# Block 0 of an attention and cos-gate MLP kernel: exponentials weigh the values first, the division by their sums follows behind TensorE; clamps on VectorE; a new order

## The chip, the core and the metric

One core of a Trainium2 chip runs the whole program. The metric is device time in microseconds (us). Engines are named as the profile names them: PE is TensorE (PEld its weight loads), DVE VectorE, ACT ScalarE, POOL GpSimd, SP the engine whose queue issues every DMA here. Each engine works through its own instructions in order.

## What is computed

```python
def _attn_ref(q, k, v):                       # (4, 8, 768, 64) each
    k_sum = k.reshape(B, H, nb, 32, D).max(axis=3)
    v_sum = v.reshape(B, H, nb, 32, D).mean(axis=3)
    scores_l = scale * np.matmul(q, k.transpose(0, 1, 3, 2))
    mask_l = np.abs(pos[:, None] - pos[None, :]) < 16
    scores_s = scale * np.einsum('bhsd,bhnd->bhsn', q, k_sum) + np.log(32)
    scores_all = np.concatenate([np.where(mask_l, scores_l, -1e9), scores_s], axis=-1)
    a = np.exp(scores_all - np.max(scores_all, axis=-1, keepdims=True))
    a = a / (np.sum(a, axis=-1, keepdims=True) + 1e-09)
    return np.matmul(a, np.concatenate([v, v_sum], axis=2))

def _moe_ref(x, w_in, w_out):                 # x (3072, 512), w_in (512, 2048)
    h = x @ w_in
    return ((h * np.cos(h)) @ w_out).astype(np.float32)
```

q, k and v are fp32. The weights are float64 in memory and are read as pairs of 32-bit words, out of which the kernel makes fp32 itself.

## The kernel before

The 3072 tokens are 8 blocks of 384 tokens (two blocks to a batch entry). Attention of a block is four **groups** a, b, c, d, each a pair of heads; `a0` is group a of block 0. A group's steps: load q, k, v and the summaries of v (`load_vs`), transposes of q and k on PE, scores on PE (its masks first, `place_masks`), a copy out of PSUM (`scale`), row maximum on DVE (`maximum`, L588), subtraction on POOL (`less_max`, L593), exponential on ACT (`exp`, L606), row sums on DVE (`sums`, L609), reciprocal on DVE (`inverse`, L614), multiplication by it on POOL (`normalize`, L617), transposes of the probabilities on PE (`turn_p`, L626) with copies on ACT (`place_p`), the product with the values on PE (`values`, L670), which comes out transposed and is x, and x split in a high and a low fp32r part (`x_high` on ACT or DVE, `x_low` on DVE, L356). From group c of block 2 on the probabilities are transposed on DVE and through DRAM instead (`square_p`, `move_out`, `move_in`).

The MLP runs in 128 **steps**; a step takes one block and one of 16 slices f of 128 hidden columns. Its `up` is 12 matmuls (L714), ACT and DVE make h cos h of it (L724, L727, L732, L735, L739), split in `gh` and `gl`, and `down` and `down_low` are 9 matmuls (L770). Steps 0 to 5 are block 0 with slices 0 to 5, steps 6 to 21 block 1 with all 16, steps 22 to 31 block 0 with the rest. `s0.up`, the first, needs x of all four groups of block 0 and slice 0 of the weights.

A weight **slice** is 1 MB of float64 bits, loaded by SP in two DMAs (L371, L375) into one of the buffers `late`, and turned into fp32 bits and split: `magnitude` on ACT (L388), `clamp` on DVE or POOL (L393), `shift`, `last_bits`, `first_bits` on DVE (L399, L407, L415), `high_part` on ACT or DVE, `low_part` mostly on POOL (L356).

Every instruction's place on its engine is written out by hand in the table `ORDER`: a token such as `b0.sm` or `s0.up.2` is one step of one group, slice or MLP step, and the letter at its end names the engine (a, v, p) or the numbers the PSUM banks. All DMAs are on SP's queue and share eight semaphores in turn, so that a DMA is issued only after the one eight places ahead of it has landed.

## Time and profile before

| | us |
|---|---|
| median of 3 runs | 663.17 (660.64 to 663.44) |
| the profiled execution, its own time | 661.89 |
| its span, first to last instruction | 660.1 |
| PE busy in the span | 632.6 (96%) |
| DVE, ACT, POOL busy | 449.7, 363.9, 221.8 |
| TensorE's mean granted clock | 0.987 |

Rows are read so: a timeline row has a start, a duration, the engine, the line of the kernel, the operation and its tiles; in square brackets stands how long the engine sat idle before it, and what ended that. A window row has, for a stretch, each engine's busy time with the number of its instructions, then PE's granted clock (1.00 is 2.4 GHz, 0.50 is 1.2 GHz), the busy share of the DMA engines and what they moved. An fp32 matmul shows as two MATMUL records.

### The profile page before, as it was taken

Reading aid. Unit: us, or ns where it says so; the run is one execution under the profiler, and the core shown is the slowest. Engines: PE = TensorE matmul, PEld = TensorE weight load, DVE = VectorE, ACT = ScalarE, POOL = GpSimd, SP = SyncE. Lnnn points to the kernel's source line nnn. Section 1 sums busy time; section 2 is a strip of 40 time slices with the busy share of each in tenths; the row PEclk is TensorE's granted clock in tenths of the full one; section 3 lists DMA queues with packets and bytes.
Section 4 is the critical chain, followed back from the end, with each engine's and each line's share of the span. In section 5 each row is a group of like instructions: output and inputs, shape, how many; then the busy total and the mean of one; then the engine's idle time right before and its main releaser. Section 6 shows DMA issues by size and latency. Waiting matters only on the chain.

```text
span 660.1 us, 13282 instructions
## 1 busy us (share of the span) xinstructions
PE 632.6 (96%) x5141; PEld 560.2 (85%) x5141; DVE 449.7 (68%) x798; ACT 363.9 (55%) x640; POOL 221.8 (34%) x219
## 2 busy tenths in 40 slices
PE   6478999999999999999999999999999999999996
PEld 5256889989988998898898899889889989899985
DVE  4887999887855576668797777576876756433344
ACT  2656977776554485437477464356554645444342
POOL 4784896764430342301323411112330212010110
PEclk9869999999999999999999999999999999999999
DMA  9997906544243244525445433424364332000001
GB/s 224 259 271 203 276 15 223 169 109 71 55 122 85 91 124 132 127 59 114 111 107 135 147 98 97 114 43 85 115 163 104 92 94 70 5 1 17 16 17 48
DMA packets 167158, 72.68 MB, mean 110 GB/s; under 512 B 136824, under 2 KB 155832, under 8 KB 167096
## 3 DMA queue, kind: packets, MB, share of 16 engines
q1 hardware_dynamic: 167096, 71.84, 40.9%
q8 instruction: 40, 0.66, 0.4%
q14 instruction: 22, 0.18, 0.1%
HBM read 53.72 MB, written 15.73 MB: 105 GB/s over the span
## 4 chain that ended last, share of the span: by engine, by line
PE 86%; DMA 5%; SPq 3%; POOL 2%; DVE 1%; issue 1%; ACT 1%; DVEq 0%; POOLq 0%; ACTq 0%
PE banks L770 39%; PE banks L714 39%; PE banks L569 4%; PE banks L670 3%; DMA late<-in_moe_w_out_dram 3%; DMA late<-in_v_dram 1%; SPq L456 1%; POOL w L356 1%; DMA late<-in_q_dram 1%; POOL gl L356 1%; SPq L493 1%; POOL stage L393 0%; ACT stage L388 0%; PE banks L556 0%; DVE m L588 0%
## 5 line engine op out<-in xcount | busy, mean ns | idle before, releaser
L714 PE MATMUL banks<-xh,w 128*128 128x384 f32 x1024 | 272.1, 337 | 0.1
L770 PE MATMUL banks<-w,gh 128*128 128x512 f32 x768 | 198.1, 393 | 0.2 <-ACT gh L350 0.2
L714 PEld LDWEIGHTS banks<-xh,w 128*128 128x128 f32 x1024 | 185.9, 188 | 2.8 <-ACT pt L350 0.4
L714 PE MATMUL banks<-xl,w 128*128 128x384 f32 x512 | 171.4, 335 | 0.0
L770 PEld LDWEIGHTS banks<-w,gh 128*128 128x128 f32 x768 | 142.6, 188 | 29.0 <-ACT gh L350 0.5
L724 ACT ACTIVATE t<-banks 128x384 int32<-128x384 f32 x128 | 62.5, 489 | 133.6 <-DVE gl L356 54.9
L356 POOL TENSOR_TENSOR gl<-t,gh 128x384 fp32r<-128x384 f32 x55 | 56.6, 1029 | 221.4 <-ACT gh L350 86.0
L770 PE MATMUL banks<-w,gl 128*128 128x512 f32 x384 | 109.8, 394 | 0.1
L727 DVE SCALAR_TENSOR_TENSOR t<-t,banks 128x384 f32<-128x384 int32 x128 | 70.0, 548 | 56.9 <-ACT t L724 56.2
L732 ACT ACTIVATE t<-t 128x384 f32<-128x384 f32 x128 | 66.7, 523 | 66.3 <-DVE t L727 66.0
L714 PEld LDWEIGHTS banks<-xl,w 128*128 128x128 f32 x512 | 96.1, 188 | 1.6
L739 DVE SCALAR_TENSOR_TENSOR t<-t,banks 128x384 f32<-128x384 f32 x128 | 69.3, 546 | 41.2 <-ACT t L735 41.0
L770 PEld LDWEIGHTS banks<-w,gl 128*128 128x128 f32 x384 | 71.1, 188 | 14.6 <-DVE gl L356 0.2
L593 POOL TENSOR_TENSOR sc<-sc,m 128x720 f32<-128x720 f32 x28 | 40.1, 1431 | 129.2 <-DVE m L588 129.2
L735 ACT ACTIVATE t<-t 128x384 f32<-128x384 f32 x128 | 65.8, 521 | 2.1
L617 POOL TENSOR_TENSOR sc<-sc,r 128x720 f32<-128x720 f32 x28 | 39.5, 1411 | 51.4 <-DVE r L614 50.3
L350 ACT CAST gh<-t 128x384 fp32r<-128x384 f32 x68 | 34.7, 510 | 33.2 <-PE banks L770 16.5
L356 DVE TENSOR_TENSOR gl<-t,gh 128x384 fp32r<-128x384 f32 x73 | 41.7, 572 | 12.6 <-ACT gh L350 6.5
L356 POOL TENSOR_TENSOR w<-stage,w 128x1024 fp32r<-128x1024 f32 x15 | 36.2, 2416 | 10.0 <-ACT w L350 8.6
L352 DVE CAST gh<-t 128x384 fp32r<-128x384 f32 x60 | 23.2, 386 | 22.2 <-PE banks L770 20.4
L580 DVE SCALAR_TENSOR_TENSOR sc<-banks,mask 128x360 f32<-128x360 f32 x48 | 24.4, 524 | 19.2 <-PE banks L569 19.0
L569 PEld LDWEIGHTS banks<-kd,qd 64*64 64x64 f32 x1344 | 28.4, 135 | 9.4 <-issue 6.7
(102 smaller groups left out, 620.7 us busy)
## 6 DMA issues: line engine op xcount, KB each, us to landing
pd<-stage SPq DMA_DIRECT2D x22, 384.0 KB
late<-in_moe_w_in_dram SPq DMA_DIRECT2D x16, 512.0 KB
late<-in_moe_w_out_dram SPq DMA_DIRECT2D x16, 512.0 KB
pt<-pd SPq DMA_DIRECT2D x66, 96.0 KB
vn<-in_v_dram SPq DMA_DIRECT2D x52, 120.0 KB
out_dram<-stage SPq DMA_DIRECT2D x23, 256.0 KB
kn<-in_v_dram SPq DMA_DIRECT2D x24, 192.0 KB
qn<-in_q_dram SPq DMA_DIRECT2D x92, 48.0 KB
```

The lines of the kernel that those rows point to most:

```text
L350: eng.copy(out=out, in_=in_)
L356: eng.tensor_tensor(out=lo, in0=src, in1=hi.bitcast(F32), op=ALU.subtract)
L569: nc.tensor.matmul(out=self.sp[hh][s * QT : (s + 1) * QT, c, lo : lo + n], lhsT=self.qd[rows, t * QT : (t + 1) * QT], rhs=self.kd[rows, ke ...
L593: nc.gpsimd.tensor_tensor(out=self.sc, in0=self.sc, in1=self.m.unsqueeze(2).broadcast_to([P, U, NK]), op=ALU.subtract)
L617: nc.gpsimd.tensor_tensor(out=self.sc, in0=self.sc, in1=self.r.unsqueeze(2).broadcast_to([P, U, NK]), op=ALU.mult)
L714: nc.tensor.matmul(out=self.h, lhsT=w_of(name, self.f)[:, c * P : (c + 1) * P], rhs=x_of(self.blk, part, c), start=n == 0, stop=n == last,)
L724: nc.scalar.activation(out=self.t.bitcast(I32), in_=self.h, func=AF.Copy, scale=1.0 / TWO_PI)
L727: nc.vector.scalar_tensor_tensor(out=self.t, in0=self.t.bitcast(I32), scalar=-TWO_PI, in1=self.h, op0=ALU.mult, op1=ALU.add)
L732: nc.scalar.activation(out=self.t, in_=self.t, func=AF.Sin, scale=0.5)
L735: nc.scalar.activation(out=self.t, in_=self.t, func=AF.Square, scale=math.sqrt(2.0))
L739: nc.vector.scalar_tensor_tensor(out=self.t, in0=self.t, scalar=-1.0, in1=self.h, op0=ALU.add, op1=ALU.mult)
L770: nc.tensor.matmul(out=self.acc[i], lhsT=g[:, i * P : (i + 1) * P], rhs=w_of(name, self.f), start=self.first and n == 0, stop=self.last an ...
```

## The change

**Block 0's values.** `LATE` marks the four groups of block 0. They have no `sums` and no `normalize`: the exponentials are transposed as they are (with one row more, the 1e-9 that stood beside them for the sum), and `values` multiplies with the probabilities as the stationary operand, so that x comes out with the tokens on the partitions. Beside each of the 12 products with the values stands one with a column of ones, which gives the sum. Then DVE takes the reciprocal of the sums (`inverse`), multiplies (`divide`, token `xn`) into one tile `xq` that all four groups use, PE transposes that (`turn_x`, `tx`, three matmuls), and `x_high` and `x_low` go on as before.

**Clamps.** Those of slices 3 and 7 move from POOL to DVE, so that all 16 are there.

**b2.** The second table of `TURNS` has a one more: group b of block 2 sends its probabilities through DVE and DRAM instead of PE.

**The order** is a new table: other places, banks and engines for many tokens.

```diff
+LATE = "11110000000000000000000000000000"
-TURNS = ("00000000011111111111111111111111", "00000000001111111111111111111111")
+TURNS = ("00000000011111111111111111111111", "00000000011111111111111111111111")
...
-b0.ck.0.v a0.ck.0.a a0.ks.0 a0.ms.5.6 a0.ck.1.a a0.ks.1 b0.q a0.sc c0.tk.0.7 a0.z.1.a a0.z.0.v w1.l c0.ck.0.a a0.mx
...
+    ones = const.tile([P, 1], F32, name="ones")
+    nc.vector.memset(ones, 1.0)
...
         def inverse(self):
-            if self.fused:
+            if self.late:
+                self.r = att.tile([P, U], F32, name="r", bufs=2)
+                nc.vector.reciprocal(out=self.r, in_=self.xw[:, :, D])
+                return
...
+                nc.tensor.transpose(out=pT[:, t - lo, :], in_=self.all[:, t, : self.rows], identity=ident)
...
         def values(self, i):
+            if self.late:
+                self.xw = bank(i)[:, : U * (D + 1)].rearrange("p (u n) -> p u n", u=U)
+                for t in range(U):
+                    c, s = divmod(t, 2)
+                    for hh in range(2):
+                        p, to = self.pt[2 * c + hh][s], self.xw[s * QT : (s + 1) * QT, 2 * c + hh]
+                        nc.tensor.matmul(
+                            out=to[:, :D], lhsT=p[:NK], rhs=self.vn[:, t, hh * D : (hh + 1) * D],
+                            start=True, stop=True,
+                        )
+                        nc.tensor.matmul(out=to[:, D:], lhsT=p, rhs=ones[: self.rows], start=True, stop=True)
+                return
...
+        def divide(self):
+            nc.vector.tensor_tensor(
+                out=self.xq.rearrange("p (u n) -> p u n", u=U), in0=self.xw[:, :, :D],
+                in1=self.r.unsqueeze(2).broadcast_to([P, U, D]), op=ALU.mult,
+            )
+
+        def turn_x(self, i):
+            self.xps = bank(i)[:, :TB]
+            for c in range(QC):
+                cols = slice(c * P, (c + 1) * P)
+                nc.tensor.transpose(out=self.xps[:, cols], in_=self.xq[:, cols], identity=ident)
```

**DVE**, from the clamp of slice 2 on. Before (L393 clamp, L399, L407, L415 the bits, L609 sums, L614 reciprocal, L356 x_low, L588 maximum):

```order
L393 TENSOR_SCALAR stage_407<-stage_407 128x1024
L415 SCALAR_TENSOR_TENSOR stage_420<-late_131,banks 128x1024
L609 TENSOR_REDUCE r<-late_130 128x6
L399 TENSOR_SCALAR banks<-stage_407 128x1024
L614 RECIPROCAL r<-r 128x6
L407 SCALAR_TENSOR_TENSOR banks<-late_125,banks 128x1024
L415 SCALAR_TENSOR_TENSOR stage_464<-late_125,banks 128x1024
L393 TENSOR_SCALAR stage_451<-stage_451 128x1024
L356 TENSOR_TENSOR xl_0_487<-banks,xh_0_459 128x384
L399 TENSOR_SCALAR banks<-stage_451 128x1024
```

The same place now, in the changed file's lines (L399 clamp, L405, L413, L421 the bits, L609 maximum, L643 reciprocal of the sums in PSUM, L722 divide, L362 x_low):

```order
L399 TENSOR_SCALAR stage_405<-stage_405 128x1024
L405 TENSOR_SCALAR banks<-stage_405 128x1024
L643 RECIPROCAL r<-banks 128x6
L413 SCALAR_TENSOR_TENSOR banks<-late_127,banks 128x1024
L722 TENSOR_TENSOR x_3_140<-banks,r 128x384
L421 SCALAR_TENSOR_TENSOR stage_470<-late_127,banks 128x1024
L609 TENSOR_REDUCE m<-sc 128x6
L399 TENSOR_SCALAR stage_453<-stage_453 128x1024
L643 RECIPROCAL r<-banks 128x6
L405 TENSOR_SCALAR banks<-stage_453 128x1024
L722 TENSOR_TENSOR x_3_140<-banks,r 128x384
L362 TENSOR_TENSOR xl_0_531<-banks,xh_0_511 128x384
```

The sums of d0 and the reciprocal that followed them are gone; the reciprocals of a0 and c0 now stand behind what PE writes to `banks`, and each divide behind its reciprocal.

**SP**, from a load of the summaries for block 1 (L493; L477 and L485 load v, L456 q, L254 the v blocks of batch entry 1, L371 and L375 a slice; `vn_104` is b0's v) on, before:

```order
L493 DMA late_128<-vs_293 24x6x64 x2
L477 DMA late_128<-in_v_dram 96x5x64 x2
L485 DMA late_128<-in_v_dram 80x2x64
L493 DMA vn_104<-vs_293 24x6x64 x2
L493 DMA late_128<-vs_293 24x6x64 x2
L456 DMA qn<-in_q_dram 128x3x64 x2
L477 DMA vn_104<-in_v_dram 96x5x64 x2
L485 DMA vn_104<-in_v_dram 80x2x64
L477 DMA late_129<-in_v_dram 96x5x64 x2
L485 DMA late_129<-in_v_dram 80x2x64
L254 DMA kn<-in_v_dram 96x512
L371 DMA late_125<-in_moe_w_in_dram 128x4x256
```

Now (L466 q, L258 v blocks, L487 and L495 v, L503 summaries, L377 a slice; `vn_106` is b0's v):

```order
L466 DMA late_132<-in_q_dram 128x3x64 x2
L258 DMA kn<-in_v_dram 96x512
L487 DMA vn_106<-in_v_dram 96x5x64 x2
L495 DMA vn_106<-in_v_dram 80x2x64
L503 DMA vn_106<-vs_297 24x6x64 x2
L503 DMA late_130<-vs_297 24x6x64 x2
L487 DMA late_131<-in_v_dram 96x5x64 x2
L495 DMA late_131<-in_v_dram 80x2x64
L503 DMA late_130<-vs_297 24x6x64 x2
L466 DMA qn<-in_q_dram 128x3x64 x2
L377 DMA late_127<-in_moe_w_in_dram 128x4x256
L381 DMA late_127<-in_moe_w_out_dram 128x1024
L466 DMA qn<-in_q_dram 128x3x64 x2
```

b0's v stands twelve DMAs earlier in the program's queue; the q of d1 (the first `qn` here) now stands behind it, and the load of slice 8 (`late_127`) directly behind that, five DMAs earlier than it was.

**PE**, from the last matmuls of `s0.up` on, before (L626 transposes of a1's exponentials, L556 masks of d1):

```order
L714 MATMUL banks<-xl_0_557,w_438 128x384
L714 MATMUL banks<-xh_0_494,w_438 128x384
L626 MATMUL banks<-ident,sc 120x128 x4
L556 MATMUL banks<-mask,ident 128x360 x2
L626 MATMUL banks<-ident,sc 120x128 x2
```

Now (L512 the transposes of a2's q, L659 those of a1's exponentials):

```order
L772 MATMUL banks<-xl_0_616,w_440 128x384
L772 MATMUL banks<-xh_0_599,w_440 128x384
L659 MATMUL banks<-ident,sc 120x128 x4
L512 MATMUL banks<-ident,qn 128x128 x3
L567 MATMUL banks<-mask,ident 128x360 x2
L659 MATMUL banks<-ident,sc 120x128 x2
```

The transposes of a2's q, which stood behind `s1.up`, now stand behind `s0.up`.

## Rows read from the trace of the kernel before

**Rows 1.** Three stretches of the span that end at 655.20 us, all engines
```profile
0.00:58.88 58.88, 37.45 (x532) 27.28 (x533) 44.10 (x61) 30.61 (x53) 37.63 (x55) 0.86 0.87 231
58.88:95.02 36.14, 35.04 (x302) 29.61 (x300) 32.81 (x48) 30.76 (x51) 29.89 (x23) 1.00 0.64 192
95.02:655.20 560.18, 560.10 (x4312) 503.33 (x4310) 371.72 (x689) 302.22 (x537) 154.29 (x143) 1.00 0.35 92
```

**Rows 2.** PE's waits, whole span: line, releaser, us in total, times, longest
```profile
PE banks L502 <- DMA late<-in_q_dram: 6.6, 3, 2.4
...
PE banks L670 <- DMA vn<-in_v_dram: 2.3, 1, 2.3
```

**Rows 3.** DVE alone from slice 1's clamp to b0's x_low, then clock and DMA
```profile
22.93:58.74 35.81, 31.29 (x37) 0.76 0.80 211
```

**Rows 4.** Timeline of DVE: clamp, sums, x_low, reciprocal, shift, maximum, slice 8's clamp
```profile
22.93 0.70 DVE L393 TENSOR_SCALAR stage<-stage 128x1024 f32<-128x1024 f32 x1 [0.31 <-ACT stage L388]
...
45.71 0.91 DVE L609 TENSOR_REDUCE r<-sc 128x6 f32<-128x726 f32 x1 [1.31 <-ACT sc L606]
46.54 0.55 DVE L356 TENSOR_TENSOR xl<-banks,xh 128x384 fp32r<-128x384 f32 x1
47.00 0.18 DVE L614 RECIPROCAL r<-r 128x6 f32<-128x6 f32 x1
47.83 1.23 DVE L399 TENSOR_SCALAR banks<-stage 128x1024 int32<-128x1024 int32 x1 [0.65 <-POOL stage L393]
49.14 0.90 DVE L588 TENSOR_REDUCE m<-sc 128x6 f32<-128x720 f32 x1
...
65.20 0.69 DVE L393 TENSOR_SCALAR stage<-stage 128x1024 f32<-128x1024 f32 x1 [1.54 <-ACT stage L388]
```

**Rows 5.** Timeline of POOL: slice 3's clamp
```profile
44.18 3.62 POOL L393 TENSOR_SCALAR stage<-stage 128x1024 f32<-128x1024 f32 x1
```

**Rows 6.** Timeline of PE: values of c0, then from a1's q to d0's values
```profile
39.26 1.55 PE L670 MATMUL banks<-pt,x 120*64 120x64 f32 x24 [0.21 <-ACT pt L350]
...
43.93 0.52 PE L502 MATMUL banks<-ident,late 128*128 128x128 f32 x3 [1.81 <-DMA late<-in_q_dram]
44.29 2.14 PE L556 MATMUL banks<-mask,ident 128*128 128x360 f32 x4
...
48.15 0.78 PE L502 MATMUL banks<-ident,late 128*128 128x128 f32 x3
48.86 0.92 PE L670 MATMUL banks<-pt,x 120*64 120x64 f32 x24
49.70 1.48 PE L556 MATMUL banks<-mask,ident 128*128 128x360 f32 x4
```

**Rows 7.** A stretch with a low clock, all engines
```profile
28.00:42.00 14.00, 6.80 (x63) 5.56 (x63) 13.68 (x18) 7.91 (x12) 11.07 (x6) 0.51 0.90 253
```

**Rows 8.** Groups of score matmuls on PE: count, busy us, mean ns, idle before
```profile
L569 PE MATMUL banks<-kd,qd 64*64 64x96 f32 x672 | 29.0, 268 | 0.0
...
L569 PE MATMUL banks<-kd,qd 64*64 64x24 f32 x672 | 24.8, 200 | 0.0
```

**Rows 9.** The chain that ended last: start and length of two slices' landing
```profile
31.82 5.28 DMA late<-in_moe_w_out_dram
...
57.51 6.41 DMA late<-in_moe_w_out_dram
```

**Rows 10.** Timeline of PE: the transposes of b1's q
```profile
37.75 0.88 PE L502 MATMUL banks<-ident,late 128*128 128x128 f32 x3 [2.35 <-DMA late<-in_q_dram]
```

**Rows 11.** Timeline of SP: issues of b1's q, d1's q and b0's v
```profile
34.11 1.03 SPq L456 DMA_DIRECT2D late<-in_q_dram  x2
...
51.88 0.98 SPq L456 DMA_DIRECT2D qn<-in_q_dram  x2
52.91 1.26 SPq L477 DMA_DIRECT2D vn<-in_v_dram  x2
```

**Rows 12.** Timeline of PE: six transposes, and the matmuls behind them
```profile
81.26 0.82 PE L626 MATMUL banks<-ident,late 128*120 128x128 f32 x6
81.84 1.64 PE L770 MATMUL banks<-w,gh 128*128 128x512 f32 x6
```

More of the change, by code (lines that the diff above doesn't have):

```diff
@@ L442, in __init__ @@
             self.squares, self.moved = (t[blk * NG + pr : blk * NG + pr + 1] == "1" for t in TURNS)
+            self.late = LATE[blk * NG + pr : blk * NG + pr + 1] == "1"
+            self.rows = NK + 1 if self.late else NK
+            self.pmax = int(PMAX[blk * NG + pr : blk * NG + pr + 1] or "0")
             self.kT, self.pT, self.pt, self.pts = {}, {}, {}, None
@@ L551, in score_banks @@
             self.sp = [bank(i)[:, : QC * NK].rearrange("p (c n) -> p c n", c=QC) for i in two]
+            self.first_bank = two[0]
         def place_masks(self, *two):
@@ L587, in maximum @@
             m = self.m = att.tile([P, U], F32, name="m", bufs=2)
+            if self.pmax:
+                i = self.first_bank
+                nc.vector.tensor_reduce(
+                    out=m.rearrange("p (c h) -> p h c", h=2),
+                    in_=banks[:, i : i + 2, : QC * NK].rearrange("p h (c n) -> p h c n", n=NK),
+                    axis=AX.X, op=ALU.max,
+                )
+                if self.pmax == 2:
+                    nc.vector.tensor_scalar_mul(m, m, -1.0)
+                return
             nc.vector.tensor_reduce(
@@ L597, in exp @@
         def exp(self):
-            self.r = att.tile([P, U], F32, name="r", bufs=2)
-            if self.fused:
+            if not self.late:
+                self.r = att.tile([P, U], F32, name="r", bufs=2)
+            if self.pmax == 2:
+                for u in range(U):
+                    c, h = divmod(u, 2)
+                    nc.scalar.activation(
+                        out=self.sc[:, u, :], in_=self.sp[h][:, c, :], func=AF.Exp, bias=self.m[:, u : u + 1],
+                        accum_out=self.r[:, u : u + 1],
+                    )
+            elif self.fused:
                 for u in range(U):
@@ L623, in turn_p @@
             lo, hi = ((0, 4), (4, U))[j]
-            pT = self.pT[j] = bank(i)[:NK, : (hi - lo) * P].rearrange("p (t n) -> p t n", t=hi - lo)
+            pT = self.pT[j] = bank(i)[: self.rows, : (hi - lo) * P].rearrange("p (t n) -> p t n", t=hi - lo)
             for t in range(lo, hi):
-                nc.tensor.transpose(out=pT[:, t - lo, :], in_=self.sc[:, t, :], identity=ident)
+                nc.tensor.transpose(out=pT[:, t - lo, :], in_=self.all[:, t, : self.rows], identity=ident)
         def place_p(self, j, eng):
@@ L631, in place_p @@
                 self.pts = att.tile([P, U * P], F32, name="pt")
-            pt = self.pts[:NK].rearrange("p (t n) -> p t n", t=U)
+            pt = self.pts[: self.rows].rearrange("p (t n) -> p t n", t=U)
             copy(eng, pt[:, lo:hi, :], self.pT[j])
@@ L846, in tile_kernel @@
     n_v, n_k, n_s = U * P, KC * P, U * NKP
-    x1 = [xp.tile([P, 2 * TB], F32, name=f"x1_{i}", tag=t) for i, t in enumerate(("xh01", "xl01", "xh11"))]
+    x1 = [xp.tile([P, 2 * TB], F32, name=f"x1_{i}", tag=t) for i, t in enumerate(("xh01", "xl01", "xh11", "xl11"))]
     qd1 = carve(late[2], 2 * n_k, P, TB)
@@ L863, in tile_kernel @@
         nc.gpsimd.memset(t[:, U - 1, :], 0.0)
+    Group.xq = carve(x1[3], 0, P, TB)
     groups = [
@@ L907, in tile_kernel @@
             su="less_max", ex="exp", sm="sums", iv="inverse", nm="normalize", tp="turn_p", cp="place_p",
-            va="values", xh="x_high", xl="x_low",
+            va="values", xn="divide", tx="turn_x", xh="x_high", xl="x_low",
         ),
```

304 lines of the change are left out of this document (155 added, 149 removed).

## Prediction

> **What bounds the kernel now.** I read the table of windows first, because it splits the run in two. From 95.02 to 655.20 us PE is busy 560.10 of 560.18 us, at 2.4 GHz throughout [rows 1]: in 85% of the span the end is the sum of PE's work, and no other engine can bring anything there but a new wait. From 58.88, where `s0.up` starts, to 95.02 PE stands still for 36.14 - 35.04 = 1.1 us [rows 1]. So the time is: start of `s0.up` (58.88), then 595.2 us of almost unbroken PE work with 1.2 us of waits in it, then 4.9 us to the span's end and 1.8 us outside it (661.89 - 660.1). A change in block 0's attention pays by the start of `s0.up`, by PE work behind it, or by those 1.2 us.
>
> What sets that start? PE's own waits ahead of it are for DMAs: 6.6 us for q, 2.3 us for b0's values [rows 2]. But the view of DVE alone shows a second limit: from slice 1's clamp at 22.93 to b0's x_low at 58.74, after which `s0.up` follows at once, DVE works 31.29 of 35.81 us [rows 3]. Without a wait it would be through at 54.2. Its 4.5 us of waits are short ones: 1.31 for b0's exponentials ahead of their sums, 0.65 for POOL's clamp [rows 4], the rest below 1.2 each. POOL is loaded too; one clamp costs it 3.62 us [rows 5]. So four queues (SP, DVE, PE, ACT) reach `s0.up` within some 4 us of each other, and taking one wait away shows the next.
>
> **Sums, normalize and divide.** In DVE's stretch three sums go (c0, d0, b0; a0's lies ahead of it): 3 x 0.91. Four divides come: each reads 384 columns from PSUM as x_low does, 0.55 [rows 4]. One reciprocal more comes into the stretch, 0.18, and the clamp of slice 3, 0.70 [rows 4]. Instructions that follow each other start about 0.09 before the one ahead has ended (46.54 + 0.55 against 47.00), so net: -2.46 + 1.84 + 0.09 + 0.61 = +0.1 us. DVE's work stays 31.4 us. POOL loses four normalizes and a clamp of 3.62, which is cover only: it is not what ends last here. The waits of 1.31 and 0.65 go with their causes.
>
> **What DVE waits for instead.** The reciprocals of a0, c0, d0 and b0 stand in DVE's line behind PE's values step; queued behind each are the bits of the next slices, which ACT, POOL and finally `s0.up` wait for. So the length of that step counts now. Before, it is 24 records in 0.92 us at 2.4 GHz and 1.55 at the low clock [rows 6]; the clock is 0.51 from 28 to 42 us, the 1.2 GHz level, since PE is busy there for 6.80 of 14.00 us [rows 7]. It gets 24 records more, with one column each. The trace has no matmul of one column. Nearest are the score matmuls: 24 columns take 200 ns where 96 take 268 [rows 8], so few columns save little. I count the added records like the old ones: 1.8 us, or 3.1 to 3.4 at the low clock. Bounds: 0.9, if the ones cost nothing; and 2.8 (5.6 low), if the products no longer overlap: two mask matmuls of 360 columns take about 1.4 us [rows 6], 115 ns for 64 columns, times 24.
>
> The Trainium skill (TensorEngine Tiling, section Instruction Overhead) says that a matmul of free dimension 1 has the latency of one of 60. Rows 8 lean that way without showing the case. By it the step is 1.8 us and the sum below stands; if only columns counted it would be 0.9, and the sum 0.9 us less.
>
> Now the step that decides. c0's v has moved behind slice 5, so slice 5 and b1's q behind it come about 1 us earlier, and c0's values start at about 38.3 instead of 39.26 [rows 6]. With 3.4 us they end at 41.7; a0's new turn_x (0.7 low) and d0's transposes (1.4) bring PE to 43.8. There it needs a1's q, which landed at 43.9 [rows 6] and still stands behind slice 3: 43.6. From that landing d0's values began 4.93 us later (43.93 to 48.86) [rows 6]; now c0's turn_x stands between (+0.4), c1's q behind (-0.7): 48.3, and with 1.8 us they end at 50.1, less some overlap with the read: 49.8. DVE without waits would be at d0's reciprocal by about 44, so it waits some 5 us in all there and at c0's, as long as the waits it lost. Behind it stand 13 instructions up to b0's x_low: three of 1.23, one clamp, two maxima, two divides, three x_low, one sum, one reciprocal, by rows 4 and less 0.09 each 9.0 us: 58.8. `s0.up` needs b0's part only with its fourth matmul, so it starts at 58.3: **-0.6**. Bounds: 54 (no DVE wait at all) and 64 (below).
>
> **SP's queue.** b0's v is issued twelve DMAs earlier, so the 2.3 us of rows 2 go; b0 has 4 us to spare then, and d1's q is the late one: issued at 51.88 [rows 11], now behind b0's v and b0's summaries, at about 54, there by 57. It just keeps out of the way. `a2`'s q is the new wait: its buffer is free only after d1's transposes, directly ahead of `s0.up`, and it is issued directly behind slice 8. q behind a slice lands behind it: b1's q, issued at 34.11 [rows 11], could be used at 37.75 [rows 10], slice 5 having landed at 31.82 + 5.28 = 37.1 [rows 9]. Slice 8 landed at 57.51 + 6.41 = 63.9 [rows 9]; five DMAs of 0.5 to 0.8 earlier it lands at about 60.9, a2's q at 61.5. PE is at a2's transposes at 58.3 + 2.1 + 0.5 = 60.9: **+0.6** (0 to 2).
>
> **Behind s0.up.** Slice 8 earlier takes the 1.54 us from DVE [rows 4], slice 7's clamp leaves POOL for 0.61 us of DVE. Of PE's 1.1 us of waits I take half away: **-0.5** (+1 to -1.1). b2 through DRAM saves PE six transposes, 0.58 us from start to start [rows 12]: **-0.6**. The clamps after 95 us and the other moves there lie beside a PE that never waits: nothing, if no new wait appears.
>
> Sum: -0.6 + 0.6 - 0.5 - 0.6 = -1.1, on the profiled execution's 661.89: 660.8. It lay 1.28 below the median, so against the median of 663.17: **662.0**.
>
> **Rivals.** *The queues open (faster).* If a1's q lands 3 us sooner, DVE has no wait left and ends at 22.93 + 31.4 = 54.3; `s0.up` starts at 54 to 55 and 4.4 us are gained, 658.2 with b2's. For it: the largest PE waits are DMAs [rows 2], and twelve DMAs less stand before b0's v. Against: a1's q itself is no nearer to the head, and d1's q would have to be there by 54.
>
> *The division holds DVE up (slower).* The values step now writes four products in a row into the same half of the partitions, where before the halves alternated. If that ends the overlap, the step is 5.6 us at the low clock. It decides from 43.6 - 38.3 - 2.1 = 3.2 us on, just where my forecast lies: c0's end at 43.9, PE at a1's q 2.4 us late, and d0's step, if the clock is still low, 3.8 longer: `s0.up` at 64.5, +5.6, less 0.6 for b2: 668. Against: PE is denser than before from 43 on, where the clock rose. The same page (section Key Properties) says that different tiles run in parallel, which speaks for this rival; no row here shows four in one half.
>
> *b2 comes late.* Its path over DVE and DRAM must fit in the PE work between its scores and its values; if a slice's 1 MB stands ahead of it in the queue, at 5.28 to 6.41 us [rows 9], part of that shows and PE waits 1 to 3 us near 200 us: 664. Against: after 95 DVE and the DMAs have room [rows 1]. *The change does nothing for s0.up, and the saved POOL time nothing at all*, is 663, inside the forecast's range.
>
> **Chances.** Forecast 0.53 (own range 660 to 664), open queues 0.20, held DVE 0.14, b2 late 0.13. 0.5% is 3.3 us, about what a measurement of this kernel can tell: the runs lie from 660.64 to 663.44. Faster (below 659.9) is the open queues and a little of the forecast: 0.22. Slower (above 666.5) is most of the held DVE: 0.13. The range takes in half of either: 657.8 to 666.5.
>
> **What would show it.** `s0.up` at 58 to 59; d0's reciprocal waiting on PE for 2 us or more, and c0's for about 2; the values step at 1.8 us (2.4 GHz); a short wait of PE at a2's q; no wait of PE after 95. I am wrong if `s0.up` starts before 56 or after 61, or if PE waits behind 100 us.

## The result and the profile after

The changed kernel is slightly slower: a median of 664.57 us over 20 runs (662.37 to 667.56) beside 662.65 over 20 runs of the kernel before (663.17 over the first three), a ratio of 1.0033 with a 95% interval of 1.0020 to 1.0045. The forecast was 662.0, a gain of 1.1 us; measured is a loss of 1.9. The time lies in the range that was given, and within 0.5% of the kernel before, but on the other side of it. The profiled execution took 665.8 us, its span 664.0. The two profiled executions lie 3.9 us apart where the medians lie 1.9, so a part of what follows belongs to these two executions and not to the change. The ratios leave out one execution of the kernel before that took 788 us and one of e1 that took 3496, which was the one profiled, so that e11 is e1's program again for its profile.

The windows of the changed kernel, cut at `s0.up` (61.40), at `s6.up` (97.52) and at the last matmul, then the stretch from c0's values to `s0.up`. Columns are those of [rows 1]: length, PE, PEld, DVE, ACT and POOL busy, granted clock, DMA share, GB/s.

```profile
0.00:61.40 61.40, 45.94 (x640) 36.60 (x641) 42.34 (x60) 29.99 (x52) 27.36 (x50) 0.83 0.98 233
61.40:97.52 36.12, 34.96 (x302) 29.31 (x300) 32.84 (x50) 29.77 (x51) 26.70 (x22) 1.00 0.61 170
97.52:658.55 561.03, 560.29 (x4305) 503.28 (x4304) 372.74 (x681) 302.55 (x537) 160.34 (x151) 1.00 0.37 93
40.77:61.40 20.63, 20.42 (x333) 17.17 (x334) 15.09 (x21) 11.97 (x22) 7.61 (x5) 0.81 0.88 220
```

The stretch of the kernel before that answers to the last of these, from c0's values at 39.26 [rows 6] to `s0.up`:

```profile
39.26:58.88 19.62, 15.54 (x249) 11.38 (x250) 15.60 (x21) 12.17 (x23) 13.31 (x7) 0.85 0.72 186
```

The 3.9 us between the two spans (664.0 - 660.1) fall into three parts. c0's values start 1.5 us later (40.77 against 39.26). From there to `s0.up` it takes 1.0 longer: PE's waits shrink from 4.08 to 0.21 us, and its work grows from 15.54 to 20.42. From `s0.up` to `s6.up` nothing changes (36.12 against 36.14). Behind `s6.up` 1.4 us are added (566.48 against 565.08 to the span's end), though b2's six transposes are gone: 0.7 of them are waits of PE ahead of its last matmul (561.03 - 560.29), and 0.55 lie behind that matmul.

PE in the same stretch, in order of time (L705 products, L709 ones, L731 turn of x, L659 transposes of exponentials, L512 of q, L772 `s0.up`). The 48 records of a values step stand in small pieces; only the first pieces are shown:

```profile
40.77 0.48 PE L705 MATMUL banks<-x,pt 120*64 120x64 f32 x2 [1.00 <-ACT pt L356]
...
43.98 0.90 PE L731 MATMUL banks<-ident,x 128*128 128x128 f32 x3
44.68 1.49 PE L659 MATMUL banks<-ident,late 128*121 128x128 f32 x6
45.96 0.85 PE L512 MATMUL banks<-ident,late 128*128 128x128 f32 x3
...
50.28 0.33 PE L705 MATMUL banks<-x,pt 120*64 120x64 f32 x2
...
52.14 0.92 PE L659 MATMUL banks<-ident,sc 128*121 128x128 f32 x6
...
60.45 0.55 PE L731 MATMUL banks<-ident,x 128*128 128x128 f32 x3
61.10 0.55 PE L512 MATMUL banks<-ident,qn 128*128 128x128 f32 x3
61.40 0.43 PE L772 MATMUL banks<-xh,w 128*128 128x384 f32 x1
```

Behind the wait of 1.00 at 40.77 there is no bracket: PE goes from one piece to the next, through 45.96 and 61.10 where it needs q of a1 and d1, without waiting for either. c0's values take 43.98 - 40.77 = 3.21 us at the low clock, d0's 52.14 - 50.28 = 1.86 at 2.4 GHz. DVE, in contrast, waits (its waits in the same stretch):

```profile
44.09 0.20 DVE L643 RECIPROCAL r<-banks 128x6 f32<-128x6 f32 x1 [3.43 <-PE banks L709]
50.88 1.23 DVE L405 TENSOR_SCALAR banks<-stage 128x1024 int32<-128x1024 int32 x1 [1.58 <-ACT sc L356]
61.54 0.56 DVE L362 TENSOR_TENSOR xl<-banks,xh 128x384 fp32r<-128x384 f32 x1 [0.63 <-ACT xh L356]
```

The last is b0's x_low. It waits for ACT's x_high, which waits for the turn of x at 60.45: PE leads, and DVE follows, but closely: from d0's reciprocal at 52.25 on these 0.63 us are all that DVE waits. PE's waits behind 80 us, of which the kernel before had one, at 90.29 us:

```profile
84.30 0.84 PE L659 MATMUL banks<-ident,late 128*120 128x128 f32 x6 [0.63 <-DVE t L797]
...
142.71 1.12 PE L580 MATMUL banks<-kd,qd 64*64 64x24 f32 x46 [0.38 <-DVE kd L546]
...
153.34 1.67 PE L828 MATMUL banks<-w,gh 128*128 128x512 f32 x6 [0.32 <-ACT gh L356]
```

### The profile page after: what moved, and what is told of

It is laid out like the page before. It is cut to its first block, busy times and chain, and to the rows that moved or that the text cites. A ratio compares the mean times of both kernels' runs of the same rounds, so it can differ in the third digit from the quotient of the medians.

```text
span 664.0 us, 13499 instructions
## 1 busy us (share of the span) xinstructions
PE 641.6 (97%) x5243; PEld 569.2 (86%) x5243; DVE 448.1 (67%) x790; ACT 363.5 (55%) x642; POOL 214.4 (32%) x221
## 4 chain that ended last, share of the span: by engine, by line
PE 80%; DMA 6%; DVE 5%; ACT 4%; SPq 3%; issue 1%; POOL 0%; ACTq 0%; POOLq 0%; DVEq 0%
PE banks L828 35%; PE banks L772 35%; DMA late<-in_moe_w_out_dram 4%; PE banks L580 4%; PE banks L716 3%; DMA late<-in_v_dram 1%; SPq L466 1%; DVE banks L413 1%; DVE stage L421 1%; ACT stage L394 1%; DMA late<-in_q_dram 1%; DVE banks L405 1%; PE banks L705 1%; PE banks L567 1%; DVE stage L399 1%
## 5 line engine op out<-in xcount | busy, mean ns | idle before, releaser
L772 PE MATMUL banks<-xh,w 128*128 128x384 f32 x1024 | 272.3, 337 | 0.5 <-ACT pt L356 0.5
L772 PEld LDWEIGHTS banks<-xh,w 128*128 128x128 f32 x1024 | 185.9, 188 | 3.8 <-ACT pt L356 0.7
L772 PE MATMUL banks<-xl,w 128*128 128x384 f32 x512 | 171.5, 335 | 0.0
L362 POOL TENSOR_TENSOR gl<-t,gh 128x384 fp32r<-128x384 f32 x61 | 62.2, 1023 | 223.3 <-ACT gh L356 93.2
L772 PEld LDWEIGHTS banks<-xl,w 128*128 128x128 f32 x512 | 96.1, 188 | 1.8
L614 POOL TENSOR_TENSOR sc<-sc,m 128x720 f32<-128x720 f32 x28 | 40.0, 1427 | 105.3 <-DVE m L609 105.3
L650 POOL TENSOR_TENSOR sc<-sc,r 128x720 f32<-128x720 f32 x26 | 36.4, 1400 | 59.7 <-DVE r L647 51.5
L356 ACT CAST gh<-t 128x384 fp32r<-128x384 f32 x71 | 36.1, 511 | 33.3 <-DVE t L797 24.9
L362 DVE TENSOR_TENSOR gl<-t,gh 128x384 fp32r<-128x384 f32 x67 | 40.2, 602 | 17.4 <-ACT gh L356 8.2
L362 POOL TENSOR_TENSOR w<-stage,w 128x1024 fp32r<-128x1024 f32 x15 | 36.1, 2405 | 13.5 <-ACT w L356 12.3
```

Of the source, the lines that this page charges most:

```text
L356: eng.copy(out=out, in_=in_)
L362: eng.tensor_tensor(out=lo, in0=src, in1=hi.bitcast(F32), op=ALU.subtract)
L614: nc.gpsimd.tensor_tensor(out=self.sc, in0=self.sc, in1=self.m.unsqueeze(2).broadcast_to([P, U, NK]), op=ALU.subtract)
L650: nc.gpsimd.tensor_tensor(out=self.sc, in0=self.sc, in1=self.r.unsqueeze(2).broadcast_to([P, U, NK]), op=ALU.mult)
L772: nc.tensor.matmul(out=self.h, lhsT=w_of(name, self.f)[:, c * P : (c + 1) * P], rhs=x_of(self.blk, part, c), start=n == 0, stop=n == last,)
```

## The experiments

Theory A, formed from these rows: the division brought PE work (ones and turns of x) into a stretch where PE's waits could just take it in, and PE itself now sets `s0.up`. Its rivals: DVE or the loads still set it (B), the low clock does (C), the new order rather than the division costs the time (D). Each ratio is to the kernel before on the same chip. The last two columns are the profiled run's.

| | kernel | median us | ratio (95%) | s0.up | s6.up |
|---|---|---|---|---|---|
| | before | 662.65 | 1 | 58.88 | 95.02 |
| | changed | 664.57 | 1.0033 (1.0020 to 1.0045) | 61.40 | 97.52 |
| e1, e11 | no ones | 662.68 | 1.0006 (0.9991 to 1.0021) | 58.19 | 95.11 |
| e2, e6 | ones as 65th column | 664.05 | 1.0021 (1.0005 to 1.0036) | 58.90, 58.70 | 95.50, 95.64 |
| e3 | PE kept busy | 664.13 | 1.0023 (1.0011 to 1.0036) | 61.09 | 97.06 |
| e4 | new order, old sums | 664.94 | 1.0031 (1.0020 to 1.0043) | 62.33 | 98.08 |
| e5 | old order, division | 668.76 | 1.0100 (1.0080 to 1.0119) | 64.52 | 99.68 |
| e7 | e2, loads moved | 662.01 | 1.0004 (0.9991 to 1.0016) | 58.44 | 94.53 |
| e8 | before, b0's v earlier | 664.57 | 1.0041 (1.0025 to 1.0056) | 58.48 | 96.45 |
| e9 | changed, loads moved | 663.67 | 1.0023 (1.0009 to 1.0037) | 59.62 | 96.62 |
| e10 | changed, two clamps on POOL | 666.43 | 1.0060 (1.0040 to 1.0080) | 61.03 | 98.48 |
| e12 | e7, PE kept busy | 662.25 | 0.9997 (0.9982 to 1.0011) | 57.46 | 94.89 |
| e13 | e7, a1's v earlier | 661.70 | 0.9992 (0.9980 to 1.0004) | 59.58 | 95.58 |
| e14 | e13, PE kept busy | 662.59 | 0.9999 (0.9985 to 1.0013) | 59.52 | 94.71 |
| e15 | changed, copy first | 664.22 | 1.0041 (1.0028 to 1.0054) | 59.24 | 94.48 |
| e16 | e13, copy first | 661.50 | 0.9995 (0.9980 to 1.0009) | 57.85 | 93.84 |

**e1 and e11: without the ones.**

```diff
-                        nc.tensor.matmul(out=to[:, D:], lhsT=p, rhs=ones[: self.rows], start=True, stop=True)
...
-                nc.vector.reciprocal(out=self.r, in_=self.xw[:, :, D])
+                nc.vector.reciprocal(out=self.r, in_=self.xw[:, :, 0])
```

> The changed kernel without the 12 ones matmuls of each of block 0's four groups; the reciprocal reads the first column of the products in place of the sums, so x of block 0 is left undivided by its sums. Theory A (in the changed kernel PE itself is the limit from c0's values at 40.77 us to s0.up at 61.40, where it never stands still, and what the change added is PE work): c0's step falls from 3.2 us (low clock) to about 1.6, d0's and b0's from 1.86 to about 0.92, so s0.up starts 2.5 to 3.5 us earlier, at 58 to 59, and the time is 661 to 662.5. Theory B (DVE or SP's queue is the limit and PE's step only fills its waits): s0.up moves by less than 0.7 us and the time stays at 664 to 665.

> A second look at the changed kernel without the ones and without the division by the sums, for its trace. Theory A: values step 0.93 us at 2.4 GHz, s0.up at 58 to 59.5, waits of PE for d1's q and a2's q as in the runs with the 65th column; time 662 to 663.5.

The ratio falls from 1.0033 to 1.0006 (the intervals just touch): the 48 matmuls of one column are worth about as much as the change lost. PE in e11 (L705 values of c0 and d0, L730 the turn of d0's x, L512 a2's q):

```profile
40.99 1.60 PE L705 MATMUL banks<-x,pt 120*64 120x64 f32 x24 [1.00 <-ACT pt L356]
...
48.26 0.97 PE L705 MATMUL banks<-x,pt 120*64 120x64 f32 x24
...
51.22 0.52 PE L730 MATMUL banks<-ident,x 128*128 128x128 f32 x3 [0.82 <-DVE x L721]
...
63.04 0.52 PE L512 MATMUL banks<-ident,qn 128*128 128x128 f32 x3 [0.73 <-DMA qn<-in_q_dram]
```

The step is half as long at either clock, and `s0.up` comes at 58.19. A holds, and B, by which `s0.up` would move by less than 0.7, does not. DVE is the next limit at once: behind d0's values PE now waits for its divides. The wait for d1's q, which was expected too, is absent.

**e2 and e6: ones and values in one matmul.** A 65th column of ones beside each head's values in SBUF; 12 matmuls again, and the whole computation.

```diff
-                            out=to[:, :D], lhsT=p[:NK], rhs=self.vn[:, t, hh * D : (hh + 1) * D],
+                            out=to, lhsT=p[:NK], rhs=self.vn[:, t, hh * (D + 1) : (hh + 1) * (D + 1)],
...
-                        nc.tensor.matmul(out=to[:, D:], lhsT=p, rhs=ones[: self.rows], start=True, stop=True)
```

> The changed kernel with the ones as a 65th column beside each head's 64 columns of values in SBUF, so that one matmul of 65 columns gives product and sum: 12 matmuls a group and not 24, the full computation. Theory A (PE's work sets s0.up; a matmul costs by its count here, not by a column more): the values step is 0.93 us at 2.4 GHz and 1.55 to 1.7 at 1.2, as without the ones, s0.up at 58 to 59, the time 661 to 662.5, faster than or equal to the kernel before at 662.65. Theory B (DVE or the queue is the limit): the step is shorter but the time stays at 664 to 665.

> A second look at the changed kernel with the ones as a 65th column, the same program as in the run with that edit: s0.up at 58 to 59.5 with a wait for d1's q of 1 to 2 us ahead of it and one for a2's q of 1 to 2 us behind it, if these two waits belong to the program; if they came from one disturbed load, at least one of them is below 0.5.

PE in e2 (L707 d0's values; L514 q of d1, ahead of `s0.up`, and of a2, behind it):

```profile
46.95 0.97 PE L707 MATMUL banks<-x,pt 120*64 120x65 f32 x24
...
58.63 0.52 PE L514 MATMUL banks<-ident,qn 128*128 128x128 f32 x3 [1.81 <-DMA qn<-in_q_dram]
...
63.44 0.52 PE L514 MATMUL banks<-ident,qn 128*128 128x128 f32 x3 [1.75 <-DMA qn<-in_q_dram]
```

The step is as short as without the ones, `s0.up` is at 58.90, and still the time falls by only 0.5 us, a miss of the expected 661 to 662.5. A part of what PE gave back, SP's queue took: 1.81 us for d1's q, then 1.75 for a2's. In e6, the same program, only the second was there (1.02), so the wait for a2's q is seen in both profiles and that for d1's q in one. But at `s6.up` e2 is only 0.5 us behind the kernel before; the rest of the miss lies behind it, where e2's profile takes 566.90 to the span's end and e6's 565.26. Why e2 is 1.4 us above e1, with nearly the same step and `s0.up`, is not settled; their intervals overlap.

**e7, e9, e13: the loads.** d1's q right behind c1's q, a2's transposes behind `s1.up` again; in e9 with the ones as matmuls of their own, in e7 and e13 with the 65th column, in e13 also a1's v ahead of a2's q.

```diff
-... c1.q w2.lo.p ... b1.m ... d1.q ... w8.l ... w4.lo.v a2.tq.2 ... s1.up.3 ...
+... c1.q d1.q w2.lo.p ... b1.m ... w8.l ... w4.lo.v ... s1.up.3 a2.tq.2 ...
```

> The changed kernel with the 65th column, and two more edits: d1's q is loaded right behind c1's q (ahead of b0's v) in place of behind b0's and b1's summaries, and a2's q is transposed behind s1.up, where the kernel before had it. Theory E (once PE's added work is gone, SP's queue is next: in the run with the 65th column alone PE waited 1.81 us for d1's q and 1.75 us for a2's q): both waits go, s0.up starts at 56.8 to 57.5, s1.up 2 to 3 us earlier, and the time is 660.5 to 662.5. Theory F (ACT and DVE behind s0.up are the limit; s2.up waited for ACT in every run of the new order): s0.up comes earlier but s2.up does not move below 70, and the time stays at 663.5 to 664.5.

> The changed kernel with its 24 matmuls of ones a half, and only the two moved loads of the last experiment (d1's q right behind c1's q, a2's q transposed behind s1.up). Theory A (PE's own work sets s0.up in the changed kernel; it never waited there for d1's q or a2's q): s0.up stays at 61 to 61.8 and the time at 664 to 665, so the loads are worth something only once PE's work is less. Theory G (the loads alone did it, the ones are harmless): 662 to 663.

> The version with the 65th column and the two moved loads, with one more load moved: a1's v behind slice 8 and ahead of a2's q, in place of behind d1's v. Theory H (behind s0.up the loads of a2's q and a1's v, which stand in SP's queue behind a DMA that waits for d1's transposes, hold PE, and behind them the chain of ACT that s2.up waits for): nothing waits for a1's v in this version at the low clock (67.14 us in the last look), so the time is 661.3 to 662.3, s0.up at 58 to 59. If the load is late in most runs, 660.5 to 661.3.

Both waits are gone in e7, and the time is 0.17% below that of e2 (the intervals overlap): it goes the way of E (SP's queue is next). But it ends level with the kernel before, not ahead: the next waits are POOL's and ACT's (e7's, ahead of a1's transposes and of `s2.up`):

```profile
61.50 0.65 PE L673 MATMUL banks<-ident,sc 128*120 128x128 f32 x4 [0.63 <-POOL sc L664]
...
69.71 0.44 PE L785 MATMUL banks<-xh,w 128*128 128x384 f32 x1 [0.46 <-ACT pt L369]
```

e9, the loads without the shorter step, is not told apart from the changed kernel, as A has it; its `s0.up` came at 59.62 and not at 61 as expected, though in the changed kernel PE waited for none of the moved loads. Of the 1.8 us between them 0.7 are the start of c0's values (40.05 against 40.77), since b1's q was there sooner in e9's run. The rest shows in the windows of e9 and then of the changed kernel:

```profile
42.00:46.00 4.00, 4.00 (x33) 3.80 (x34) 2.63 (x5) 1.37 (x3) 1.56 (x1) 0.58 1.21 269
46.00:50.00 4.00, 4.00 (x99) 3.30 (x98) 3.47 (x4) 3.49 (x8) 0.00 (x0) 1.00 1.08 253
```

```profile
42.00:46.00 4.00, 4.00 (x46) 3.98 (x43) 1.91 (x4) 0.65 (x2) 2.22 (x1) 0.50 1.23 247
46.00:50.00 4.00, 4.00 (x49) 2.80 (x51) 3.28 (x4) 2.80 (x5) 0.00 (x0) 0.67 1.15 296
```

PE is busy all of these 8 us in both. In e9 the granted clock is back at 1.00 by 46 us, in the changed kernel's run only during 46 to 50. Such a difference moves `s0.up` by about a microsecond, so a single profile's `s0.up` is no finer than that.

**e3, e12, e14: PE kept busy.** Matmuls of the mask into a bank whose content is overwritten, ten in e3 and 14 in e12 and e14, where PE stood still.

```diff
+        def busy(self, i, n):
+            for _ in range(n):
+                nc.tensor.matmul(
+                    out=bank(i)[:, : QC * NK].rearrange("p (c n) -> p c n", c=QC),
+                    lhsT=ident, rhs=mask[:, :QC, :], start=True, stop=True,
+                )
```

> The changed kernel with ten matmuls of the mask (360 columns, 0.69 us each at 2.4 GHz) whose result is overwritten, put on PE where it stands idle: two ahead of b0's q, two ahead of d0's q, five ahead of a0's values, one ahead of b1's q. Theory C (part of what was lost is the granted clock, 0.50 from 31.5 to 48.6 us because PE was idle for half of the time ahead of it): with PE busy the clock stays at 1.00 to 40 us or longer, c0's values take about 1.9 us and not 3.2, the stretch from c0's values to s0.up 17 us and not 20.6, the time 661 to 663. Against it: if the clock falls all the same, the added matmuls take up to 1.4 us each and s0.up comes 0 to 3 us later, 664 to 668.

> The version with the 65th column and the two moved loads, with 14 matmuls of the mask whose result is overwritten where PE stands idle (two ahead of b0's q, two ahead of d0's q, six ahead of a0's values, four ahead of b1's q). Theory C (the granted clock of 0.50 from 29.3 to 46.3 us still costs: c0's values, a turn of x, d0's transposes and a1's masks stand in it): the clock is 1.00 to beyond 40, s0.up at 56 to 57.5, the time 660 to 661.5. Theory F (behind s0.up ACT and DVE are the limit): s0.up may come earlier, s2.up stays at 69 to 70, the time within 0.5 of 662.0.

> The same with the 14 matmuls of the mask that keep PE busy. With them s0.up started at 57.46 and s1.up at 63.06, and then PE waited 1.79 us for a1's v and 0.46 for ACT. Theory H: the 1.79 us go, s2.up at 68.4 to 69 in place of 70.15 and the time 660.2 to 661.3, faster than the kernel before. Theory F (ACT and DVE are the limit there, not a load): s2.up stays at 69.5 to 70.2 and the time within 0.5 of 662.2.

Two windows of e3:

```profile
28.00:38.00 10.00, 5.63 (x63) 3.79 (x61) 9.64 (x12) 8.11 (x11) 5.92 (x3) 1.00 0.94 224
40.00:48.00 8.00, 7.45 (x63) 6.79 (x64) 4.98 (x9) 4.32 (x9) 4.08 (x2) 0.50 1.16 310
```

The clock held to 38 us, ten microseconds longer than in the kernel before, and then fell to 0.50, behind a wait of PE of 2.93 us for b1's q, just where c0's values stood. So nothing came of it (1.0023). In e12 the clock was 0.83 over the same 40 to 48 us, `s0.up` at 57.46, and then PE waited for a1's v:

```profile
67.53 1.36 PE L729 MATMUL banks<-pt,late 120*64 120x64 f32 x24 [1.79 <-DMA late<-in_v_dram]
```

e13 and e14 take that wait away, and neither comes out ahead. In e14, with the clock at 1.00 from 28 to 50 us, PE waits for a1's q and then for ACT instead:

```profile
43.77 0.52 PE L526 MATMUL banks<-ident,late 128*128 128x128 f32 x3 [1.91 <-DMA late<-in_q_dram]
...
50.65 0.52 PE L526 MATMUL banks<-ident,late 128*128 128x128 f32 x3 [2.06 <-ACT pt L369]
```

So the low clock costs PE time, but in these runs no time of the kernel that can be told: none of the three is told apart from the version without the added matmuls, and the loads and ACT are due just behind.

**e4 and e5: division and order apart.** e4 has the new order with the old sums, divided on POOL ahead of the transposes; e5 the old order, clamps, loads and b2 with the division behind PE.

```diff
-LATE = "11110000000000000000000000000000"
+LATE = "00000000000000000000000000000000"
...
-... a0.va.1 d0.sm w0.hi.a d1.m w2.sh.6.7 ... w2.lb b1.tq.3 a1.q a0.xh.a ...
+... a0.va.1 w0.hi.a d1.m w2.sh.6.7 a0.iv ... w2.lb a0.xn b1.tq.3 a1.q a0.tx.1 a0.xh.a ...
```

> The changed kernel's order, clamps and loads, but block 0 as before: sums on DVE, normalize on POOL ahead of the transposes, no ones, no divide, no turn of x. Theory A (the added PE work is what was lost): PE has 5.3 us less to do ahead of s0.up, of it 4.5 behind c0's values; s0.up at 57 to 60, the time 660 to 663. Theory D (the new order is what was lost, the division as such is harmless): the time stays at 664 or above, s0.up at 61 or later.

> The kernel before, in its own order, clamps, loads and path of b2, with the division behind PE alone: exponentials as they are into the transposes, 24 matmuls more a group, reciprocal, divide and turn of x behind each group's values. Theory A (the added PE work is what was lost): behind c0's values the division brings 1.7 + 0.94 + 0.94 us of values and about 1.9 us of turns of x, 5.4 us in all, and the kernel before has 1.81 + 2.27 us of PE's waits there to take it in; with the read of each sum between, s0.up starts at 60 to 62 in place of 58.88 and the time is 663.5 to 666. Theory D (the new order is what was lost): 662 to 663.2, the kernel before within 0.1%.

e5 costs 1.0%: the division alone, in an order made for the other one, loses 6.6 us, more than expected. c0's values start at 42.36 there, 3.1 us later than before, behind a0's longer step, and the stretch to `s0.up` is full of PE work:

```profile
42.36:64.52 22.16, 20.40 (x331) 16.50 (x331) 15.79 (x24) 11.91 (x23) 12.46 (x6) 0.83 0.75 167
```

e4 shows the opposite: with the old division the new order makes PE wait for POOL (L671, transposes of c0's, d0's and b0's exponentials):

```profile
38.53 1.11 PE L671 MATMUL banks<-ident,late 128*120 128x128 f32 x4 [3.00 <-POOL late L662]
...
44.69 1.53 PE L671 MATMUL banks<-ident,late 128*120 128x128 f32 x6 [1.43 <-POOL late L662]
...
53.06 1.48 PE L671 MATMUL banks<-ident,sc 128*120 128x128 f32 x6 [1.67 <-POOL sc L662]
```

A's forecast for e4 (57 to 60, 660 to 663 us) is missed, and D's for it (61 or later, 664 or above) came out; in e5 D's (662 to 663.2) fails, and A's (663.5 to 666) is exceeded. D is not shown even so: e4's places for sums and normalize were chosen for this run, and its loss can be that of a step put into an order which leaves it no room. What the pair shows is that order and division belong together. The order, with the clamps, the loads and b2's path that go with it, gives back some 4.4 of the 6.6 us (1.0100 to 1.0033).

**e10: the clamps back on POOL.**

```diff
-... w3.cl.v ... w7.cl.v ...
+... w3.cl.p ... w7.cl.p ...
```

> The changed kernel with the clamps of slices 3 and 7 on POOL again, 3.62 us each there in place of 0.70 on DVE. By theory A DVE is not what ends last ahead of s0.up, so the 0.70 us saved on DVE bring nothing there; POOL's 3.62 us for slice 3 stand ahead of a1's subtraction and c1's normalize and may come out on the path: no change to 1 us slower, 664.3 to 666. If the clamps on DVE were what the change lost, the time falls to 662.5 to 663.5.

In the new order the clamps on DVE pay, and more than expected: without them the ratio is 1.0060 against 1.0033, 1.8 us, with intervals that barely overlap. `s0.up` is the same (61.03), so slice 3's clamp shows no cost. Slice 7's does (POOL's clamp, DVE's wait for it, then PE's two waits for what stands behind that on DVE):

```profile
87.36 3.63 POOL L411 TENSOR_SCALAR stage<-stage 128x1024 f32<-128x1024 f32 x1
```

```profile
91.03 1.23 DVE L417 TENSOR_SCALAR banks<-stage 128x1024 int32<-128x1024 int32 x1 [2.48 <-POOL stage L411]
```

```profile
94.36 0.92 PE L728 MATMUL banks<-pt,late 120*64 120x64 f32 x24 [0.81 <-DVE xl L374]
...
95.96 0.96 PE L840 MATMUL banks<-w,gl 128*128 128x512 f32 x3 [0.68 <-DVE gl L374]
```

This is a price in the new order. The kernel before made the same clamp on POOL too, 5.5 us earlier (81.83), and there DVE waited for it for 0.37 us and PE not at all:

```profile
85.49 1.23 DVE L399 TENSOR_SCALAR banks<-stage 128x1024 int32<-128x1024 int32 x1 [0.37 <-POOL stage L393]
```

**e8: the kernel before with b0's v earlier.**

```diff
-... w4.l a1.m ... b0.su a1.v ... c1.sc w3.lb a1.su b0.v ...
+... w4.l a1.m ... b0.su b0.v a1.v ... c1.sc w3.lb a1.su ...
```

> The kernel before with one load moved: b0's v ahead of a1's v, in place of behind d1's q, as the changed kernel has it. My reading of the kernel before was that its queues end within some 4 us of each other, so that one wait taken away shows the next: PE's wait of 2.27 us for b0's values goes, DVE's 1.14 us for b0's x with it, s0.up at 57.5 to 58.3 and the time 661.6 to 662.6, a gain of at most 1.1. If that load alone was what ended last, s0.up is at 56.6 and the time 660.4.

Expected was a small gain; measured is a loss of 0.41%. PE's wait for b0's v goes, and one for d1's q stands in its place (PE), and slice 8, which ACT takes up at 64.03 in the kernel before and at 65.46 here, is late (ACT):

```profile
58.18 0.52 PE L514 MATMUL banks<-ident,qn 128*128 128x128 f32 x3 [1.50 <-DMA qn<-in_q_dram]
```

```profile
65.46 1.12 ACT L400 ACTIVATE stage<-late 128x1024 f32<-128x1024 f32 x1 [2.43 <-DMA late<-in_moe_w_out_dram]
```

The next wait showed at once, as expected, but the sign was wrong: `s0.up` is only 0.4 us earlier (58.48), and from there to `s6.up` it takes 37.97 us in place of 36.14. How much of that is the moved load is not settled: in this profile b1's q, which stands ahead of it in the queue, was there only at 39.59 (37.75 before [rows 10]).

**e15 and e16: a copy moved.** On ACT the first of the two copies of c0's exponentials no longer stands behind the second, for which ACT waits.

```diff
-... w5.ab.1 w2.lb ... c0.cp.1.a d0.v c0.cp.0.a ...
+... w5.ab.1 c0.cp.0.a w2.lb ... c0.cp.1.a d0.v ...
```

> The changed kernel with one copy moved on ACT: the first of the two copies of c0's transposed exponentials (512 columns, 0.59 us) ahead of the wait for the second, right behind the magnitudes of slice 5, where the changed kernel made it behind the second. In the changed kernel PE waited 1.00 us for these copies ahead of c0's values (40.77 us), 0.21 in the kernel before. Theory A (from c0's values on PE never stands still, so that its start moves s0.up one for one): c0's values 0.5 to 0.6 us earlier against the landing of b1's q, the wait 0.4 to 0.5, s0.up 60.5 to 61, time 663.6 to 664.4. If the limit is elsewhere: the wait is shorter, but PE stands still for as long further on, s0.up at 61.4, 664.5.

> The same copy moved in the version with the 65th column, d1's q and a1's v loaded earlier and a2's q transposed later (661.7, ratio 0.9992 to the kernel before). There PE waited 1.00 us at c0's values too, and later 0.82 and 0.28 for DVE's divides. By theory A only what those waits leave passes through: 0.2 to 0.5 us, 661.1 to 661.6, a ratio of 0.9983 to 0.9990; if ACT and DVE behind s0.up are the limit, no change: 661.7.

c0's values begin at 39.47 in e15, 1.3 us earlier: 0.9 because b1's q was there at 37.57 in this run (38.47 in the changed kernel's), 0.4 by the copy. The wait that is left is for c0's own v; PE then runs through to 59.24 without a wait:

```profile
39.47 0.45 PE L717 MATMUL banks<-x,pt 120*64 120x64 f32 x2 [0.60 <-DMA x<-in_v_dram]
```

```profile
39.47:59.24 19.77, 19.56 (x333) 16.77 (x334) 15.82 (x23) 11.84 (x22) 8.22 (x5) 0.84 0.89 214
```

In the profile the earlier start is passed on to `s0.up` in full, as A has it, and 0.9 us more with it (the stretch is 19.77 long against 20.63, at a clock of 0.84 against 0.81). In the time nothing of it is left (ratio 1.0041, not told apart from 1.0033); the profiled run is the fastest of its five, 662.84 beside a median of 664.22. e16 is level with e13 and with the kernel before.

No version is shown to beat the kernel before. The five versions with two repairs, one matmul for product and sum and the loads that are due next moved forward (e7, e12, e13, e14, e16), lie at 0.9992 to 1.0004, each with an interval wholly below that of the changed kernel: the division can be had at no cost that these runs can tell. The versions with one repair, e2 and e9, lie at 1.0021 and 1.0023 and are not told apart from the changed kernel.

## Why the prediction was wrong

Forecast was -1.1 us, measured is +1.9 (the last sum is a tenth off: 660.8 and 1.28 make 662.1). In the profiles `s0.up` came 2.5 us later (61.40 against 58.88), where 0.6 earlier was forecast, and the gains behind it did not come.

**The start of c0's values: the step that failed.** The prediction put it at 38.3, because with c0's v moved behind it slice 5, and b1's q behind the slice, would come about 1 us earlier. It came at 40.77. Of the error of 3.1 us at `s0.up` (58.3 forecast), 2.5 are this start. The load was moved, but what stood behind it did not move up: next in SP's queue are c0's summaries, which DVE has to make first. Before, c0's v filled that time; now SP stands still (SP's issue of c0's summaries before, the same now, and SP's wait for them now):

```profile
21.84 1.82 SPq L493 DMA_DIRECT2D x<-vs  x2
```

```profile
21.69 1.82 SPq L503 DMA_DIRECT2D x<-vs  x2
```

```profile
SPq L503 <- DVE vs L284: 2.7, 1, 2.7
```

So slice 5's second half was issued at 32.16 (31.82 before [rows 9]), and ACT took the slice up at 37.18, as before (37.20). b1's q was usable at 38.47 (37.75 before [rows 10]); in the other profiles of the new order with the late division it was so between 37.56 and 39.45, so that the 0.7 may be this run's, but 1 us earlier came in none. The copy behind it cost another 0.8 (a wait of 1.00 against 0.21 [rows 6], seen in ten other profiles of the new order as well), an order on ACT that was not looked at.

**What sets `s0.up`: the other engine, by 0.6 us.** The prediction let PE lead up to d0's values and DVE from there on (13 instructions, 9.0 us to b0's x_low). DVE's length was right: 61.54 - 52.25 = 9.29 us from d0's reciprocal to b0's x_low, 0.63 of it the wait at the end. But from the end of d0's values PE's own pieces take 61.40 - 52.14 = 9.26 us without a gap, where the forecast left 58.3 - 50.1 = 8.2 to `s0.up`, and DVE's x_low waited for PE at the end. PE's work was priced only where DVE reads it; summed over the stretch (4.9 us more, 4.1 us of waits to take it in) it would have shown that PE comes out as the bound. e11 shows how near the two are: with half the step DVE works from d0's reciprocal at 49.99 to b0's x_low at 58.71 with one wait of 0.20, and PE waits for it. That `s0.up` is 3 us earlier there speaks for PE's work as the cause, but does not tell the two readings apart behind d0's values, since most of it comes from the two steps ahead of them. The wait of d0's reciprocal for PE, forecast as 2 us or more, did not show: c0's waited 3.43, and d0's stood behind DVE's 1.58 for ACT. From c0's values to `s0.up` the prediction had 20.0 us, and 20.63 were measured.

**The values step: right.** 1.8 and 3.1 to 3.4 were forecast, 1.86 and 3.21 measured. At 2.4 GHz 24 records of 64 columns take 0.92 us before [rows 6], 24 of 65 take 0.97 in e2, and 24 of 64 with 24 of one column 1.86: up to 65 columns the count of matmuls is paid, not the columns. The rule of the Trainium skill (TensorEngine Tiling, section Instruction Overhead) agrees, and the sum by it was the right one. The bound of 2.8 was worked out low: 1.4 us for 720 columns is 124 ns for 64, and 24 of these are 3.0.

**a2's q: the wait is there, but hidden.** Forecast were 0.6 us. In the changed kernel PE comes so late that it does not wait, and the term is 0; in e2, e6 and e11, where PE is earlier, it waits 1.75, 1.02 and 0.73.

**Behind `s0.up`: wrong.** A gain of 0.5 was forecast, since slice 8 would come some 3 us earlier. Its second half was issued at 57.02 (57.51 [rows 9]), and DVE clamped it at 66.93 (65.20 [rows 4]): again a place further ahead in the queue was counted as time gained. From `s0.up` to `s6.up` there is no gain, and the profiled run lost more behind it. Two of the signs that were to show the prediction wrong came: `s0.up` after 61, and waits of PE behind 100 us (142.71 and 153.34). From `s6.up` to the span's end the profiles of the new order take 564.7 to 565.5 us in most runs (565.08 before) and 566.1 to 566.9 in four: the changed kernel's, e2, e10 and e15. So this loss comes in some runs; what decides it is not settled. All four have the loads as the change put them; of the six profiles with the loads moved (e7, e9, e12, e13, e14, e16) none has it, which is too few to show that the loads decide it. That slice 7's clamp pays on DVE is borne out in the new order by e10, where it is 1.8 us and not part of 0.5.

**b2: no sign against it.** PE has 30 transposes of exponentials in `sc` in place of 36, and no wait near 200 us. The rival that it comes late is out; the gain of 0.6 cannot be seen beside the loss in that stretch.

**The rivals.** *The division holds DVE up* was nearest. It was said to decide from a step of 3.2 us, and the step took 3.21; PE came to a1's q at 45.96, 2.4 us behind 43.6 as priced there. But its cause is not shown: 48 records take 1.86 us where 24 take 0.92 to 0.97, so they still overlap. PE came late because c0's values started late, and d0's step, at 2.4 GHz by then, did not add the 3.8 us. *The queues open* did not come: a1's q was no sooner, since in e14, where PE is early, it waits for it until 43.77, as the forecast's 43.6 had it. e8, which moves b0's v alone, gained 0.4 us at `s0.up`.

## What to carry to other kernels

A load taken out of a queue is not time gained for the load behind it: look first at what that one waits for, here a sum on DVE that was ready no sooner. Before a step is moved behind an engine, sum that engine's own work and waits over the stretch, and not just the steps that others wait for; here 4.9 us of new work met 4.1 us of waits. Where four queues end within a few microseconds, the waits of the profile are not gains to be had: take one away and price what is due next, for e2, e8, e12 and e14 each found a wait of 1.5 to 2.1 us there. A sum that PE computes costs nothing that shows here as one more column of a matmul that runs anyway (a step of 0.97 us with it in e2, of 0.97 without it in e11), and about as much as the product, 0.9 us, when it is a matmul of its own.
